# Attention and a two-layer FFN on one core: the first four pairs of heads by 128-partition scores, mask products and transposes, in a new table of steps

## The chip, the core and the metric

One core of one Trainium2 chip. The metric is the device time of one execution, in microseconds (us); lower is better. The engines: PE is TensorE, which multiplies matrices and loads its weights ahead; DVE (VectorE), ACT (ScalarE) and POOL (GpSimd) work element by element; SP issues loads and stores. The on-chip memories are SBUF and, for results of TensorE, eight banks of PSUM.

## The reference

B, H, S, D = 8, 8, 576, 64. Heads 0 to 3 attend to the 32 latest positions, heads 4 to 7 to every fourth of the 128 latest.

```python
scores = scale * np.matmul(q, k.transpose(0, 1, 3, 2))          # scale = 1/8
mask_plain = (rel >= 0) & (rel < window)                        # window 32
mask_dil = (rel >= 0) & (rel < window * dilation) & (rel % dilation == 0)
scores = np.where(masks[None, :, :, :], scores, -1000000000.0)
attn = np.exp(scores - np.max(scores, axis=-1, keepdims=True))
attn = attn / (np.sum(attn, axis=-1, keepdims=True) + 1e-09)
x = np.matmul(attn, v) -> (4608, 512)                           # 4608 tokens, 8 heads x 64
h = x @ w_in                                                    # w_in 512 x 2048
g = np.where(h >= 1, h, np.where(h <= -1, 0.0, (h + 1) ** 2 / 4))
return g @ w_out                                                # w_out 2048 x 512
```

## The kernel before

**Attention.** The 64 heads of the batch are 32 pairs; a pair's 128 rows are one chunk c of the 512 columns of x. The queries of a head stand in 18 blocks of 32, each against 64 keys. For a pair, 36 matmuls (72 instructions) make the scores (S, L179), on 96 partitions by 768 elements; DVE adds the mask (`mask`, L188 to L210); then come the maximum (`max`, L221, DVE), its subtraction (`sub`, L225, POOL), the exponential (`exp`, L229, ACT), the sum (`sum`, L232, DVE), plus epsilon (`eps`, L236, ACT), the reciprocal (`rcp`, L240, DVE) and the product with it (`mul`, L244, POOL). The probabilities are transposed, for pairs 0, 1 and 3 by 12 plain matmuls with a unit matrix (T, L275) that ACT copies out of PSUM (`cp`, L285), for the others by DVE (`tr`, L258), and multiplied with the values (V: 36 matmuls for pairs 0, 1 and 3, L314; 12 of 128 keys for the others, L324).

**The FFN.** x is split into a high and a low part (`hi`, ACT, L295; `lo`, DVE, L299), as is each weight. A tile is 512 tokens; there are 9, each of 16 chunks f of 128 hidden columns. Layer 1 makes h of a chunk by 12 products of 128x128 by 512 (L458: four chunks c by high-high, low-high, high-low); then clamp (DVE, L468), square (`sq`, ACT, L474), larger of the two (`mx`, DVE, L478), high part `gh` (ACT, L485) and low part `gl` (DVE, L490); layer 2 adds 12 products into acc (L504; `o`).

**Weights** come in eight blocks of w_in and eight of w_out, wi0 to wi7 and wo0 to wo7, of two chunks each, as raw 64-bit words (1024 KB a load). ACT takes their top bytes (B, L423) and the scaled rest (P, L416), DVE joins them (J, L429), ACT casts the high part (D, L436) and POOL subtracts for the low part (E, L440).

**Order.** Everything up to the ninth pair and the first tile is written out by hand in the table FIRST: a step's name, its pair or chunk, and its part; each engine and SP runs its own instructions in that order. `const` steps are filler products on TensorE whose results nobody reads. Each raw load or pair's load is an entry of SP's queue: a pair's queries and keys are 592 KB, values 576 KB (L127) or 384 KB (L131), the mask 252 KB. From the tenth pair on a loop over chunks sets the order. BANKS gives the PSUM banks that steps of early pairs write; steps without an entry (S0, S3, V2) take the two banks called `att`. A step that writes a bank waits until the last reader of what stood there is done.

Of the kernel before, what the change touches and what calls it, by code (L numbers as in the profile page):

```python
# [37 lines left out]
lo2.0 h1.0l hi3.0 h0.0h hi3.2 h0.0l hi2.1 lo3.2 h0.1h hi3.1 lo2.1 lo3.0 P.wo0 h0.1l h0.2h lo3.1
h0.2l h0.3h D.wi1 J.wo0 h0.3l S4 qk5 raw.wo1 raw.wi3 raw.wo2 raw.wi4 raw.wo3 raw.wi5 raw.wo4 hi3.3
B.wi2 clamp0 E.wi1 h1.1h h1.1l lo3.3 h1.2h mask4 sq0 h1.2l h1.3h D.wo0 mx0 h1.3l h2.h max4 gh0 P.wi2  # L40
gl0 sub4 h2.l clamp1 h3.h sq1 J.wi2 exp4 mx1 E.wo0 D.wi2 h3.l sum4 gh1 o0.a clamp2 eps4 rcp4 sq2 gl1
mul4 o0.b P.wo1 mx2 h4.h clamp3 E.wi2 gh2 tr4.20 sq3 tr4.11 o1.a B.wo1 gl2 mx3 o0.c J.wo1 h4.l gh3
o1.b gl3 D.wo1 tr4.00 B.wi3 h5.h E.wo1 clamp4 tr4.21 P.wi3 tr4.10 h5.l tr4.01 sq4 J.wi3 o2.a P.wo2
mx4 B.wo2 V4 clamp5 D.wi3 o3.a J.wo2 hi4.0 E.wi3 o2.b hi4.1 lo4.0 hi4.2 gh4 lo4.1 lo4.2 sq5 gl4 S5
qk6 raw.wo5 raw.wi6 raw.wi7 raw.wo6 raw.wo7 D.wo2 mx5 h6.h mask5 B.wo3 E.wo2 max5 h6.l gh5 B.wi4 gl5
o3.b sub5 clamp6 P.wi4 h7.h exp5 J.wi4 P.wo3 h7.l sum5 sq6 o4.b J.wo3 eps5 D.wi4 rcp5 o5.b mx6 mul5
D.wo3 clamp7 o4.a gh6 E.wi4 B.wo4 gl6 o5.a tr5.21 sq7 tr5.01 B.wi5 E.wo3 h8.h mx7 tr5.10 gh7 tr5.00
# [16 lines left out]
def body(ctx, tc, qk, v, v2, mask, w_in, w_out, out):  # L64
# [77 lines left out]
    def constants(count, at):  # L142

        ones, wide = half_t.broadcast_to([128, 128]), half_t.broadcast_to([128, TOK])
        for _ in range(count):
            PE.matmul(out=at, lhsT=ones, rhs=wide, start=True, stop=True)  # L146
# [156 lines left out]
    def values(n, banks=None):  # L303
        hd = heads[n]
        half = NB // 2
        both, ops = banks_of(banks, f"o{n}")
        if n in EARLY:
            for i in range(half):
                for turn in range(2):
                    for part in range(2):  # L310
                        j = part ^ turn
                        r = slice(64 * part, 64 * part + 64)
                        at = 3 * (i // 3 * 2 + j) + i % 3
                        PE.matmul(  # L314
                            out=ops[part][64 * j : 64 * j + 64, QB * i : QB * i + QB],
                            lhsT=hd["v"][r, at],
                            rhs=hd["pt"][r, QB * at : QB * at + QB],
                            start=True,
                            stop=True,
                        )  # L320
        else:
            for t in range(NB // 3):
                for j in range(2):
                    PE.matmul(  # L324
# [381 lines left out]
```

## Time and profile before

| | us |
|---|---|
| median of 3 runs | 889.78 (888.92 to 890.01) |
| the profiled execution | 889.96 |
| its span in the profile | 888.2 |
| TensorE busy, of the span | 876.3 (99%) |
| DVE busy | 545.8 (61%) |
| ACT busy | 306.1 (34%) |
| POOL busy | 133.4 (15%) |
| first product of layer 1 starts | 32.73 |

The span is what the hardware profiler saw from the first instruction to the last; 1.76 us of the execution lie around it. Engines are busy side by side, so their shares do not add up; a busy TensorE may still run at a lower clock, which the profile gives as a granted clock (1.00 is 2.4 GHz, 0.50 is 1.2 GHz).

### The profile page before, as it was taken

The page shows a single profiled execution, that of the slowest core. Times are in us where ns is not written, and L with a number is a line of the kernel's source. Part 1 is how long each engine was busy: PE and PEld are TensorE (multiplying, and loading weights), DVE is VectorE, ACT ScalarE, POOL GpSimd, SP SyncE. Part 2 cuts the span into 40 slices and gives each one's busy share as a digit, 9 for nine tenths or more (in the row PEclk, how much of TensorE's full clock was granted, in tenths as well). Part 3 has the DMA queues.
Part 4 walks back from the last instruction along what each step waited for, and adds up shares of the span by engine and source line. Part 5 has one row for each costly group of instructions (what it writes and reads, how often), then busy time and mean ns, then how long its engine had stood idle before and what let it go on. Part 6 is the DMA issues. An engine that isn't in the chain of part 4 may idle for free.

```text
span 888.2 us, 15897 instructions
## 1 busy us (share of the span) xinstructions
PE 876.3 (99%) x6854; PEld 714.6 (80%) x6854; DVE 545.8 (61%) x865; ACT 306.1 (34%) x496; POOL 133.4 (15%) x84
## 2 busy tenths in 40 slices
PE   7999999999999999999999999999999999999998
PEld 4778878888888888888888888888888888888886
DVE  5799887666766666666666676666666443334333
ACT  3688643322322232232332332223223222222222
POOL 4455441101011111111110101111111000000000
PEclk9899999999999999999999999999999999999999
DMA  9577112101201021101210120102110010001001
GB/s 358 219 283 289 42 64 76 63 28 61 79 20 46 28 99 42 63 29 63 76 63 28 64 75 16 50 28 96 44 64 1 1 47 1 1 1 48 1 1 47
DMA packets 16885, 60.05 MB, mean 68 GB/s; under 512 B 1872, under 2 KB 1872, under 8 KB 14768
## 3 DMA queue, kind: packets, MB, share of 16 engines
q1 hardware_dynamic: 16816, 59.05, 18.4%
q8 instruction: 53, 0.87, 0.4%
q14 instruction: 16, 0.13, 0.0%
HBM read 49.61 MB, written 9.44 MB: 66 GB/s over the span
## 4 chain that ended last, share of the span: by engine, by line
PE 95%; DVE 2%; DMA 1%; POOL 1%; issue 1%; ACT 0%; SPq 0%; POOLq 0%; ACTq 0%
PE acc L504 44%; PE h L458 43%; PE os L337 3%; PE s L179 2%; PE os L179 1%; DMA wi_first<-qk_in 1%; PE o L324 1%; PE consts L146 1%; DVE m_wi L429 0%; DVE m_wo L429 0%; PE t L275 0%; DVE c L221 0%; POOL wi_first L244 0%; DVE gl L490 0%; DVE h L478 0%
## 5 line engine op out<-in xcount | busy, mean ns | idle before, releaser
L504 PE MATMUL acc<-wo,gh 128*128 128x512 f32 x1152 | 381.9, 392 | 0.0
L458 PE MATMUL h<-xh,wi 128*128 128x512 f32 x1152 | 358.2, 390 | 0.9 <-ACT y L474 0.7
L504 PEld LDWEIGHTS acc<-wo,gh 128*128 128x128 f32 x1152 | 216.1, 188 | 47.8 <-DVE gl L490 0.5
L458 PEld LDWEIGHTS h<-xh,wi 128*128 128x128 f32 x1152 | 216.0, 188 | 47.8 <-DVE gl L490 1.1
L504 PE MATMUL acc<-wo,gl 128*128 128x512 f32 x576 | 224.3, 389 | 0.0
L458 PE MATMUL h<-xl,wi 128*128 128x512 f32 x576 | 224.2, 389 | 0.0
L474 ACT ACTIVATE y<-y,small 128x512 f32<-128x512 f32 x144 | 104.2, 724 | 310.5 <-DVE y L468 310.3
L468 DVE TENSOR_SCALAR y<-h 128x512 f32<-128x512 f32 x144 | 99.1, 688 | 114.4 <-PE h L458 111.6
L478 DVE TENSOR_TENSOR h<-h,y 128x512 f32<-128x512 f32 x144 | 100.5, 698 | 98.4 <-ACT y L474 98.4
L490 DVE TENSOR_TENSOR gl<-h,gh 128x512 fp32r<-128x512 f32 x144 | 99.2, 689 | 54.9 <-ACT gh L485 53.3
L458 PEld LDWEIGHTS h<-xl,wi 128*128 128x128 f32 x576 | 108.2, 188 | 22.5
L504 PEld LDWEIGHTS acc<-wo,gl 128*128 128x128 f32 x576 | 108.2, 188 | 21.8
L485 ACT CAST gh<-h 128x512 fp32r<-128x512 f32 x144 | 84.5, 587 | 102.3 <-DVE h L478 99.7
L225 POOL TENSOR_TENSOR c<-c 96x768 f32<-96x768 f32 x29 | 42.7, 1473 | 443.5 <-DVE c L221 443.4
L258 DVE STREAM_TRANSPOSE pts<-c 32x384 f32<-32x384 f32 x168 | 95.3, 568 | 2.9 <-POOL c L244 0.4
L244 POOL TENSOR_TENSOR c<-c 96x768 f32<-96x768 f32 x30 | 44.2, 1473 | 76.2 <-DVE c L240 76.2
L232 DVE TENSOR_REDUCE c<-c 96x12 f32<-96x768 f32 x30 | 28.4, 947 | 38.8 <-ACT c L229 38.8
L229 ACT ACTIVATE c<-c 96x768 f32<-96x768 f32 x30 | 25.4, 845 | 46.8 <-POOL c L225 39.2
L295 ACT CAST xh<-os 128x384 fp32r<-128x384 f32 (+7 forms) x48 | 19.2, 400 | 42.0 <-DVE c L201 21.9
L337 PEld LDWEIGHTS os<-pts,v 128*64 128x64 f32 x576 | 24.5, 137 | 8.5 <-DVE gl L490 6.3
L337 PE MATMUL os<-pts,v 128*64 128x96 f32 x576 | 29.1, 250 | 0.0
L221 DVE TENSOR_REDUCE c<-c 96x12 f32<-96x768 f32 x30 | 28.3, 943 | 0.4
(81 smaller groups left out, 388.4 us busy)
## 6 DMA issues: line engine op xcount, KB each, us to landing
qk<-qk_in SPq DMA_DIRECT2D x29, 592.0 KB, 3.9
v<-v_in SPq DMA_DIRECT2D x28, 384.0 KB, 5.1
raw_wi<-w_in SPq DMA_DIRECT2D x8, 1024.0 KB, 10.6
raw_wo<-w_in SPq DMA_DIRECT2D x8, 1024.0 KB, 12.3
out<-out SPq DMA_DIRECT2D x32, 256.0 KB, 2.1
wi_first<-qk_in SPq DMA_DIRECT2D x2, 592.0 KB, 7.6
out<-outs SPq DMA_DIRECT2D x4, 256.0 KB, 2.0
wo_first<-qk_in SPq DMA_DIRECT2D x1, 592.0 KB, 9.1
```

Of the source, the lines that this page charges most:

```text
L225: engine.tensor_tensor(out=c, in0=c, in1=spread(n, 0), op=ALU.subtract)
L232: nc.vector.tensor_reduce(out=heads[n]["st"][:, 1], in_=heads[n]["c"], op=ALU.add, axis=AX.X)
L244: nc.gpsimd.tensor_tensor(out=c, in0=c, in1=spread(n, 2), op=ALU.mult)
L258: nc.vector.transpose(out=pt[r : r + 32, :, 32 * g : 32 * g + 32], in_=c[32 * g : 32 * g + 32, :, 32 * h : 32 * h + 32],)
L337: PE.matmul(out=at[64 * j : 64 * j + 64, 96 * t : 96 * t + 96], lhsT=hd["v"][:, j, t], rhs=pts[:, j, t], start=True, stop=True,)
L458: PE.matmul(out=hp, lhsT=weight("wi", f, w, slice(128 * c, 128 * c + 128)), rhs=xtile(t)[x][:, c], start=start and (c, w, x) == terms[0], ...
L468: nc.vector.tensor_scalar(out=gs[t, f][0], in0=hps[t, f], scalar1=-1.0, scalar2=1.0, op0=ALU.max, op1=ALU.min)
L474: nc.scalar.activation(out=y, in_=y, func=AF.Square, bias=half_t, scale=0.5)
L478: done.append([nc.vector.tensor_tensor(out=hp, in0=hp, in1=gs[t, f][0], op=ALU.max)])
L485: done[-1].insert(0, nc.scalar.copy(out=g_tile("gh", t, f), in_=hps[t, f]))
L490: nc.vector.tensor_tensor(out=g_tile("gl", t, f), in0=hp, in1=gh.bitcast(F32), op=ALU.subtract)
L504: PE.matmul(out=acc[m], lhsT=g[:, 128 * m : 128 * m + 128], rhs=weight("wo", f, w, slice(0, DM)), start=f == 0 and i == 0, stop=f == NF - ...
```

## The change

For the first four pairs, which all end before the first product of layer 1:

- The scores lie on 128 partitions in three groups of 192 elements, 576 per partition instead of 768 (`early_scores`). Three matmuls of a unit matrix with a mask table (`pm`) write the mask into PSUM first, and the scores are added onto it there. The table with the unit matrix (`tab0`, `tab1`) is loaded ahead of the pairs; the old mask comes later (`late`).
- DVE takes the maximum and subtracts it, straight from PSUM, in two or three operations per pair; `eps` is on DVE, and for pair 3 the product `mul3.v` too.
- T is six matmuls in TensorE's transpose mode, of 128 rows each, copied out by three operations (four of them on ACT, eight on DVE).
- V is 12 matmuls over 128 keys for every early pair; the rows of the transposed table that hold no key are set to zero at the start (seven memsets on DVE). The values are 384 KB for each pair.
- FIRST is another table. From V5 and D.wi5 on its steps stand as before; ahead of that, loads, fillers, attention of pairs 0 to 5, the splitting of x and the first chunks are in another order. o1.a now stands ahead of h4.h.

The core of the diff (of the table one line):

```diff
-EARLY = (0, 1, 3)
+EARLY = 4
...
-S0 const1.5 qk4 mask0 S1 max0 sub0 S2 const1.5 mask1.0 exp0 mask1.1 S3 const1.5 max1 mask2.1
+tab0 qk0 qk1 small49 fill2.5 fill2.5 pm0 pm1 S0 S1 max0 max1.0 max1.2 max0.1 sub0 sub0.1 max1.1 exp0
...
+    def filling(columns, at):
+
+        wide = half_t.broadcast_to([128, 128 * columns])
+        PE.matmul(out=at[:, : 128 * columns], lhsT=wide[:, :128], rhs=wide, start=True, stop=True)
...
+    def place_of(j, b):
+
+        t, r = divmod(b, 3)
+        rr = (1, 0, 2)[r]
+        return (2 * j, rr, t) if t < 4 else (1, rr, 2 * j + t - 4)
+
+    def early_tiles(n):
+
         hd = heads[n]
         if "c" not in hd:
-            hd["c"] = pool.tile([96, 832], F32, tag="c", name=f"c{n}", bufs=2)
+            hd["c"] = pool.tile([128, 832], F32, tag="c", name=f"c{n}", bufs=2)
         cc = hd["c"]
+        hd["wide"] = cc[:, :672].rearrange("p (k x) -> p k x", k=3)
+        hd["c"] = hd["wide"][:, :, QB:].rearrange("p k (r x) -> p k r x", x=KW)
+        hd["st"] = cc[:, 672:699].rearrange("p (s k r) -> p s k r", s=3, k=3)
+        nc.vector.memset(hd["wide"][:, :, :QB], 0.0)
+        if n:
+            nc.vector.memset(hd["pts"], 0.0)
+            hd["pts"] = hd["pts"].rearrange("p (u x) -> p u x", x=96)
+        else:
+            hd["pts"] = pts.rearrange("p j t x -> p (j t) x")
+
+    def early_scores(n):
+        hd = heads[n]
+        sps = hd["s"][1]
+        for j, b in [(j, 3 * t + r) for t in range(6) for r in range(3) for j in range(2)]:
+            k, rr, g = place_of(j, b)
+            r = slice(64 * j, 64 * j + 64)
+            PE.matmul(
+                out=sps[k][QB * g : QB * g + QB, KW * rr : KW * rr + KW],
+                lhsT=hd["q"][r, QB * b : QB * b + QB],
+                rhs=hd["k"][r, QB * b : QB * b + KW],
+                start=False,
+                stop=True,
+                skip_group_check=True,
+            )
...
+    def masks_first(n, banks=None):
+
+        hd = heads[n]
+        both, (one, two) = banks_of(banks, f"s{n}")
+        hd["s"] = both, (one, bank(4 + n % 2, f"sc{n}"), two)
+        ident, m = tables[0][:, :128], tables[n // 2][:, 0 if n // 2 else 128 :]
+        rest = m[:, :KW].unsqueeze(1).broadcast_to([128, 3, KW]) if n < 2 else m[:, 3 * KW :]
+        for sp, rhs in zip(hd["s"][1], (m, rest, m)):
+            o = sp[:, : 3 * KW]
+            PE.matmul(
+                out=o.rearrange("p (a x) -> p a x", x=KW) if len(rhs.shape) > 2 else o,
+                lhsT=ident, rhs=rhs if len(rhs.shape) > 2 else rhs[:, : 3 * KW],
+                start=True, stop=False, skip_group_check=True,
+            )
+
+    def halves(n, k):
+        both, sps = heads[n]["s"]
+        if k is None:
+            return slice(0, 3, 2), both[:, :, : 3 * KW].rearrange("p k (r x) -> p k r x", x=KW)
+        r, src = slice(k, k + 1), sps[k][:, : 3 * KW].unsqueeze(1)
+        return r, src.rearrange("p k (r x) -> p k r x", x=KW)
...
+    def largest(n, k=None):
+        r, src = halves(n, k) if n < EARLY else (slice(0, 2), heads[n]["c"])
+        nc.vector.tensor_reduce(out=heads[n]["st"][:, 0, r], in_=src, op=ALU.max, axis=AX.X)
+
+    def minus_largest(n, k=None):
         c = heads[n]["c"]
-        engine.tensor_tensor(out=c, in0=c, in1=spread(n, 0), op=ALU.subtract)
+        if n < EARLY:
+            r, src = halves(n, k)
+            nc.vector.tensor_tensor(out=c[:, r], in0=src, in1=spread(n, 0)[:, r], op=ALU.subtract)
+            return
+        nc.gpsimd.tensor_tensor(out=c, in0=c, in1=spread(n, 0), op=ALU.subtract)
...
     def epsilon(n):
         st = heads[n]["st"]
+        if n < EARLY:
+            nc.vector.tensor_scalar(out=st[:, 1], in0=st[:, 1], scalar1=EPS, scalar2=None, op0=ALU.add)
+            return
...
-    def divided(n):
+    def divided(n, engine=nc.gpsimd):
         c = heads[n]["c"]
-        nc.gpsimd.tensor_tensor(out=c, in0=c, in1=spread(n, 2), op=ALU.mult)
+        engine.tensor_tensor(out=c, in0=c, in1=spread(n, 2), op=ALU.mult)
...
     def transpose_pe(n, banks):
...
+
+        hd, ident = heads[n], tables[0][:, :128]
+        tps = hd["t"] = banks_of(banks, f"t{n}")[1]
+        for k in range(3):
+            for side, x in enumerate((hd["wide"][:, k, 96:], hd["wide"][:, k, :96])):
+                PE.transpose(tps[side][: x.shape[1], 128 * k : 128 * k + 128], x, ident)
+
+    def copied(n, r, engine=None):
+        rows = (slice(0, 64), slice(0, 96), slice(64, 128))[r]
+        src = heads[n]["t"][r % 2][rows, :384].rearrange("p (u x) -> p u x", x=QB)
+        dst = heads[n]["pts"][rows, :, QB * r : QB * r + QB]
+        if engine:
+            nc.vector.tensor_copy(out=dst, in_=src)
+        else:
+            nc.scalar.copy(out=dst, in_=src)
...
-        half = NB // 2
         both, ops = banks_of(banks, f"o{n}")
...
+        for t in range(NB // 3):
+            for j in range(2):
+                if n < EARLY:
+                    x = hd["pts"][:, t + (0, 8 if t < 4 else 2)[j]]
+                else:
+                    x = pts[:, j, t]
+                PE.matmul(
+                    out=ops[t // 3][64 * j : 64 * j + 64, 96 * (t % 3) : 96 * (t % 3) + 96],
+                    lhsT=hd["v"][:, j, t],
+                    rhs=x,
+                    start=True,
+                    stop=True,
+                )
         hd["o"] = list(pieces(n, both, ops))
...
-    BANKS = {"S1": (0, 1), "S2": (2, 3), "T0": (0, 1), "T1": (2, 3), "T3": (0, 1), "V0": (4, 5), "V1": (2, 3), "V3": (2, 3)}
+    BANKS = {"S1": (0, 1), "S2": (2, 3), "T0": (0, 1), "T1": (2, 3), "T2": (0, 1), "T3": (0, 1), "V0": (4, 5), "V1": (2, 3), "V3": (2, 3)}
+    QUEUES = {None: nc.sync, "a": nc.scalar}
...
+        "tab": lambda i: nc.sync.dma_start(
+            out=tables[int(i)], in_=mask4[:, 320 * int(i) : 320 + 384 * int(i)]
+        ),
+        "late": lambda _: nc.sync.dma_start(out=small[:96, : 9 * KW], in_=mask),
...
+    for n in range(EARLY):
+        heads[n] = {}
+    for n in range(1, EARLY):
+        heads[n].update(first_batch(n))
+    for n in range(EARLY):
+        early_tiles(n)
```

**SP, the loads.** From the start of the program, before and now. wi_first, wo_first, xl_first and xh_first are places of later weights and of x in which early pairs lie; 128x1184 is a pair's queries and keys, 128x2048 a weight block, v or 128x768 and 128x1152 values.

```order
L120 DMA qk_68<-qk_in 128x1184
L603 DMA small<-mask_in 96x672
L120 DMA wi_first<-qk_in 128x1184
L120 DMA wi_first_74<-qk_in 128x1184
L120 DMA wo_first_77<-qk_in 128x1184
L127 DMA v_80<-v_in 128x1152
L403 DMA raw_wi_82<-w_in 128x2048
L127 DMA wo_first<-v_in 128x1152
L131 DMA xh_first_75<-v_in 128x768
L127 DMA xl_first_78<-v_in 128x1152
```

```order
L639 DMA wi_first_68<-mask_in 128x320
L117 DMA qk_86<-qk_in 128x1184
L117 DMA wi_first_68<-qk_in 128x1184
L124 DMA xl_first_73<-v_in 128x768
L124 DMA wo_first_69<-v_in 128x768
L639 DMA wi_first_68<-mask_in 128x384
L117 DMA wi_first_70<-qk_in 128x1184
L124 DMA v_250<-v_in 128x768
L117 DMA xh_first_72<-qk_in 128x1184
L449 DMA raw_wi_370<-w_in 128x2048
L449 DMA raw_wi_456<-w_in 128x2048
L124 DMA wo_first_71<-v_in 128x768
```

Behind the pairs' loads stood one pair's values and the first weights; now the mask tables and three pairs' values stand ahead of the fourth pair, and both blocks of w_in before v2.

**DVE, the end of the early attention.** From the reciprocal of pair 1 to the splitting of x before, and from pair 3's maximum on now. wi_first_74 was pair 2 and wo_first_77 pair 3; now wi_first_70 is pair 2 and xh_first_72 pair 3. COPY rows are copies of transposes out of PSUM.

```order
L240 RECIPROCAL c_187<-c_187 96x12
L210 TENSOR_TENSOR wo_first_77<-s_271,small 96x768
L221 TENSOR_REDUCE wo_first_77<-wo_first_77 96x12
L232 TENSOR_REDUCE wi_first_74<-wi_first_74 96x12
L240 RECIPROCAL wi_first_74<-wi_first_74 96x12
L429 SCALAR_TENSOR_TENSOR m_wi_338<-m_wi_338,raw_wi_82 128x1024
L232 TENSOR_REDUCE wo_first_77<-wo_first_77 96x12
L240 RECIPROCAL wo_first_77<-wo_first_77 96x12
L258 STREAM_TRANSPOSE pts<-wi_first_74 32x12x32 x6
```

```order
L279 TENSOR_TENSOR xh_first_72<-s_288,xh_first_72 128x2x192
L279 TENSOR_TENSOR xh_first_72<-sc_289,xh_first_72 128x192
L288 TENSOR_REDUCE wi_first_70<-wi_first_70 128x9
L293 TENSOR_SCALAR wi_first_70<-wi_first_70 128x9
L341 COPY wo_first_69<-t_2_358 64x12x32
L299 RECIPROCAL wi_first_70<-wi_first_70 128x9
L288 TENSOR_REDUCE xh_first_72<-xh_first_72 128x9
L341 COPY wo_first_69<-t_2_358 64x12x32
L293 TENSOR_SCALAR xh_first_72<-xh_first_72 128x9
L299 RECIPROCAL xh_first_72<-xh_first_72 128x9
L341 COPY wo_first_69<-t_3_359 96x12x32
L303 TENSOR_TENSOR xh_first_72<-xh_first_72 128x3x192
```

The mask's addition went; subtraction, epsilon, the copies and pair 3's product came to DVE, and J.wi0 (L429, now L475) stands behind them all.

**DVE, the first chunks.** From the join of wo0 before, and from the clamp of chunk 0 now. L468/L514 is clamp, L299/L357 lo, L429/L475 J, L478/L524 mx, L203/L251 mask4, L221/L273 max4, L490/L536 gl, L288 sum4.

```order
L429 SCALAR_TENSOR_TENSOR m_wo_573<-m_wo_573,raw_wo_89 128x1024
L468 TENSOR_SCALAR y_0_642<-h_0_561 128x512
L299 TENSOR_TENSOR xl_483<-o_3_513,xh_482 128x16x2
L203 TENSOR_TENSOR c_586<-s_587,small 96x768
L478 TENSOR_TENSOR h_0_561<-h_0_561,y_0_642 128x512
L221 TENSOR_REDUCE c_586<-c_586 96x12
L490 TENSOR_TENSOR gl_0_674<-h_0_561,gh_0_670 128x512
L468 TENSOR_SCALAR y_1_681<-h_1_555 128x512
L429 SCALAR_TENSOR_TENSOR m_wi_672<-m_wi_672,raw_wi_405 128x1024
L478 TENSOR_TENSOR h_1_555<-h_1_555,y_1_681 128x512
```

```order
L514 TENSOR_SCALAR y_0_522<-h_0_486 128x512
L357 TENSOR_TENSOR xl_428<-o_3_473,xh_427 128x16x2
L357 TENSOR_TENSOR xl_428<-o_459,xh_427 128x64
L475 SCALAR_TENSOR_TENSOR m_wo_530<-m_wo_530,raw_wo_506 128x1024
L524 TENSOR_TENSOR h_0_486<-h_0_486,y_0_522 128x512
L251 TENSOR_TENSOR c_545<-s_546,small 96x768
L273 TENSOR_REDUCE c_545<-c_545 96x12
L536 TENSOR_TENSOR gl_0_606<-h_0_486,gh_0_601 128x512
L514 TENSOR_SCALAR y_1_608<-h_1_489 128x512
L475 SCALAR_TENSOR_TENSOR m_wi_603<-m_wi_603,raw_wi_527 128x1024
L524 TENSOR_TENSOR h_1_489<-h_1_489,y_1_608 128x512
L288 TENSOR_REDUCE c_545<-c_545 96x12
```

J.wo0 moved from ahead of the clamp of chunk 0 to behind it and behind two lo steps; J.wi2 stands ahead of mx1 as before.

## Rows read from the trace of the kernel before

**Rows 1.** The page's chain that ended last, share of the span by line.

```profile
PE acc L504 44%; PE h L458 43%; PE os L337 3%; PE s L179 2%; PE os L179 1%; DMA wi_first<-qk_in 1%; PE o L324 1%; PE consts L146 1%; DVE m_wi L429 0%; DVE m_wo L429 0%; PE t L275 0%; DVE c L221 0%; POOL wi_first L244 0%; DVE gl L490 0%; DVE h L478 0%
```

**Rows 2.** The stretches view: start:end, length, then each engine's busy time, granted clock, DMA.

```profile
32.73:47.75 15.02, 14.36 (x138) 11.38 (x130) 13.27 (x19) 11.34 (x20) 6.96 (x4) 1.00 0.63 247
...
60.00:600.00 540.00, 539.76 (x4354) 441.57 (x4352) 363.81 (x585) 191.09 (x312) 94.00 (x57) 1.00 0.18 62
```

**Rows 3.** The chain in order of time (start, length, what), from 33 us on.

```profile
40.97 3.90 DVE m_wi L429
...
54.47 2.72 PE h L458 x12
...
58.55 1.14 PE o L324 x24
```

**Rows 4.** The same chain up to the first h product.

```profile
18.34 1.17 PE t L275 x24
...
24.63 1.34 PE t L275 x17
...
26.23 0.91 PE t L275 x7
27.14 2.02 PE consts L146 x2
...
29.20 2.19 PE o L324 x24
...
32.80 3.62 PE h L458 x15
```

**Rows 5.** The stretches view around the start of the h stream.

```profile
26.00:31.00 5.00, 4.71 (x31) 2.92 (x32) 3.54 (x8) 1.78 (x4) 0.90 (x1) 0.50 0.58 226
31.00:32.00 1.00, 1.00 (x37) 0.78 (x34) 0.00 (x0) 0.57 (x2) 0.00 (x0) 0.56 0.00 0
32.00:33.00 1.00, 1.00 (x57) 0.96 (x50) 0.69 (x1) 1.00 (x3) 0.00 (x0) 1.00 0.00 0
```

**Rows 6.** The timeline of TensorE (start, length, line, out<-in, count, idle before): scores.

```profile
8.82 0.97 PE L179 MATMUL s<-wi_first 64*32 64x64 f32 x72 [1.13 <-DMA wi_first<-qk_in]
10.26 0.97 PE L179 MATMUL s<-wi_first 64*32 64x64 f32 x72 [0.47 <-DMA wi_first<-qk_in]
```

**Rows 7.** The timeline of DVE.

```profile
6.67 0.95 DVE L203 TENSOR_TENSOR c<-s,small 96x768 f32<-96x768 f32 x1 [5.81 <-PE s L179]
...
11.73 0.54 DVE L201 TENSOR_TENSOR wi_first<-s,small 96x384 f32<-96x384 f32 x1
...
16.93 0.22 DVE L240 RECIPROCAL c<-c 96x12 f32<-96x12 f32 x1 [1.49 <-ACT c L236]
...
21.59 0.94 DVE L232 TENSOR_REDUCE wo_first<-wo_first 96x12 f32<-96x768 f32 x1
...
28.99 1.22 DVE L429 SCALAR_TENSOR_TENSOR m_wi<-m_wi,raw_wi 128x1024 uint32<-128x1024 uint32 x1
...
36.47 0.69 DVE L468 TENSOR_SCALAR y<-h 128x512 f32<-128x512 f32 x1 [0.36 <-PE h L458]
```

**Rows 8.** The groups of DVE by line and form, 60 to 600 us.

```profile
L299 DVE TENSOR_TENSOR xl<-os,xh 128x192 fp32r<-128x192 f32 x8 | 2.8, 356 | 1.5 <-ACT xh L295 1.5
```

**Rows 9.** The timeline of POOL.

```profile
20.67 2.32 POOL L244 TENSOR_TENSOR wi_first<-wi_first 96x768 f32<-96x768 f32 x1 [0.17 <-DVE wi_first L240]
...
39.95 1.47 POOL L225 TENSOR_TENSOR c<-c 96x768 f32<-96x768 f32 x1 [1.58 <-DVE c L221]
41.38 2.41 POOL L440 TENSOR_TENSOR wo<-m_wo,wo 128x1024 fp32r<-128x1024 f32 x1
```

**Rows 10.** The timeline of ACT.

```profile
32.98 0.87 ACT L295 CAST xh<-o 128x256 fp32r<-128x256 f32 x4
33.68 1.17 ACT L416 ACTIVATE m_wo<-raw_wo 128x1024 f32<-128x1024 f32 x1
34.72 1.07 ACT L436 CAST wi<-m_wi 128x1024 fp32r<-128x1024 f32 x1
```

More of the change, by code (lines that the diff above doesn't have):

```diff
@@ L38 @@
[L38 to L47, printed above, removed]
@@ new lines @@
+sub2.0 sum1 sub2.1 eps1 sub2.2 rcp1 exp2 mul1 qk3 S3 max3 max3.1 sub3 sub3.1 T0 cp0.0 cp0.2 T1 exp3
+cp0.1 sum2 eps2 raw.wi0 B.wi0 fill3.att cp1.0.v rcp2 mul2 sum3 cp1.2.v eps3 rcp3 cp1.1.v mul3.v V0
+T2 V1 P.wi0 J.wi0 hi0.1 hi0.0 hi0.2 cp2.2 hi1.2 hi1.0 D.wi0 E.wi0 cp2.0.v cp2.1.v T3 lo0.2 lo1.0
+hi1.1 cp3.0.v cp3.2.v cp3.1.v lo1.2 lo1.1 lo0.1 lo0.0 raw.wi1 v2 V2 V3 h0.0h h1.0h B.wi1 hi3.2 hi3.0
+P.wi1 hi2.0 hi3.1 hi3.3 hi2.1 lo3.0 lo3.2 J.wi1 lo3.1 lo2.0 raw.wo0 h0.0l h1.1l h0.1l h0.2l h0.1h
@@ new lines @@
+h0.3h h1.3h h1.0l h0.2h h0.3l clamp0 B.wo0 lo3.3 lo2.1 raw.wi2 B.wi2 P.wo0 J.wo0 D.wi1 sq0 E.wi1
+h1.2l D.wo0 v4 qk4 S4 h1.1h h1.2h h1.3l h2.h late mx0 mask4 max4 gh0 P.wi2 sub4 gl0 clamp1 J.wi2
+E.wo0 h2.l h3.h o0.a h3.l o0.b raw.wo1 raw.wo3 B.wo3 sq1 exp4 mx1 sum4 clamp2 gh1 D.wi2 eps4 rcp4
+gl1 mul4 E.wi2 o1.a h4.h sq2 P.wo1 mx2 gh2 clamp3 sq3 B.wo1 gl2 o0.c o1.b h4.l mx3 gh3 J.wo1 D.wo1
+E.wo1 gl3 h5.h h5.l o2.a tr4.10 tr4.21 tr4.20 clamp4 tr4.11 tr4.00 tr4.01 raw.wi6 V4 o2.b o3.a
+raw.wo4 raw.wi3 raw.wo2 qk5 B.wi3 P.wi3 sq4 J.wi3 P.wo2 B.wo2 J.wo2 mx4 D.wi3 E.wi3 hi4.2 hi4.0
@@ new lines @@
+hi4.1 lo4.1 clamp5 lo4.0 lo4.2 S5 raw.wi4 raw.wo7 raw.wi7 raw.wo6 raw.wi5 raw.wo5 qk6 gh4 gl4 h6.h
+h6.l sq5 D.wo2 mx5 mask5 max5 E.wo2 sub5 B.wi4 gh5 P.wi4 P.wo3 clamp6 gl5 o3.b o4.a o4.b h7.h h7.l
+J.wi4 J.wo3 B.wi5 exp5 D.wi4 sq6 E.wi4 sum5 mx6 B.wo4 gh6 gl6 clamp7 h8.h o5.b h8.l o5.a D.wo3 eps5
+rcp5 mul5 E.wo3 P.wi5 sq7 mx7 tr5.20 tr5.01 tr5.10 tr5.11 o6.b J.wi5 P.wo4 gh7 B.wo5 o6.a clamp8
+tr5.00 tr5.21 gl7 D.wi5 V5 v6 J.wo4 sq8 h9.h E.wi5 hi5.2 mx8 hi5.0 hi5.1 lo5.0 gh8 lo5.1 D.wo4 h9.l
@@ L63, in body @@
 @with_exitstack
-def body(ctx, tc, qk, v, v2, mask, w_in, w_out, out):
+def body(ctx, tc, qk, v, mask, mask4, w_in, w_out, out):
     nc = tc.nc
@@ L136, in load_v @@
             for i in range(2):
-                nc.sync.dma_start(out=both[:, i].rearrange("p j t d -> p (j t d)"), in_=v2[n + i - len(EARLY)])
+                nc.sync.dma_start(out=both[:, i].rearrange("p j t d -> p (j t d)"), in_=v[n + i])
                 heads.setdefault(n + i, {})["v"] = both[:, i]
     last, done = {}, []
[L142 to L146, printed above, removed]
+    def filling(columns, at):
+        wide = half_t.broadcast_to([128, 128 * columns])
+        PE.matmul(out=at[:, : 128 * columns], lhsT=wide[:, :128], rhs=wide, start=True, stop=True)
     def small_constants(count, ats):
@@ L304, in values @@
         hd = heads[n]
-        half = NB // 2
         both, ops = banks_of(banks, f"o{n}")
[L307 to L324, printed above, removed]
-                        out=ops[t // 3][64 * j : 64 * j + 64, 96 * (t % 3) : 96 * (t % 3) + 96],
-                        lhsT=hd["v"][:, j, t],
-                        rhs=pts[:, j, t],
-                        start=True,
-                        stop=True,
-                    )
+        for t in range(NB // 3):
+            for j in range(2):
+                if n < EARLY:
+                    x = hd["pts"][:, t + (0, 8 if t < 4 else 2)[j]]
+                else:
+                    x = pts[:, j, t]
[6 more added lines that the diff above has]
+                )
         hd["o"] = list(pieces(n, both, ops))
```

144 lines of the change are left out of this document (59 added, 85 removed).

## The prediction

> **What bounds the kernel now.** I read the page's chain first: TensorE's products of the two layers, acc and h, make 87% of it [rows 1]. The stretches say where TensorE still idles. From the first h product at 32.73 us to 47.75 it is busy 14.36 of 15.02 us, and between 60 and 600 us all but 0.24 [rows 2]. So the time is the start of the h stream, plus a fixed amount of TensorE work, plus what the stream stalls. Only steps up to V5 are moved, so a gain can come only from the first 33 us, and be given back only in the stream's first stretch. There, 57 products stand before 47.75. Twelve take 2.72 us further on [rows 3], that is 0.227 each; 57 x 0.227 + S4 0.9 = 13.8, so before loses 1.2 us there.
>
> The chain of the first 33 us ends with the transposes of the fourth pair (24.63 to 27.14), filler products (2.02 us), V2 (2.19), V3, and h [rows 4]. V4, the same 24 instructions as V2, takes 1.14 us [rows 3]: V2 ran at half clock. The granted clock is 0.50 from 26 to 31 us (the 1.2 GHz level) and 1.00 again from 32, less than a microsecond ahead of h [rows 5].
>
> **The fourth pair arrives later.** Scores of pairs 1 and 2 started as their loads came, 1.44 us apart for 592 KB: 411 KB/us [rows 6]. At 10.26 us 2028 KB had come. In the new order of loads 3872 KB end with pair 3's: 10.26 + 1844 / 411 = 14.75. It is 3 us later than before, yet before made little of it: T0, next behind S3, began at 18.34 [rows 4]. S3 takes about a microsecond, as S1 did [rows 6]: 15.75. The mask's three products per pair wait for no pair's load and lie under it; bare, three of 192 columns would be 1.1 us at the price of the half-clock fillers (2.02 for two of 512 [rows 4]). The seven memsets on DVE have the idle 5.81 us ahead of 6.67 [rows 7]; they cost 3 x 1.55 + 4 x 0.2 = 5.4 at the price of 128x512 elements (0.69, so 1.55 for 1152) and stay covered, barely.
>
> **DVE then sets the pace**, fourteen operations up to pair 3's product. By the nearest rows: five of 384 elements from PSUM at 0.54 (2.70), two of 192 at 0.36 [rows 8] (0.72), three of 576 at three quarters of 0.94 (2.12), four small ones at 0.22 (0.88) [rows 7]: 6.4. Rows start 0.09 before the previous ends: less 1.2. For hand-overs I add 0.6: 5.8, ending at 21.6. J.wi0 (1.22 [rows 7]) and two copies of pair 2 (0.54 each) follow, since T3 writes the banks they read: 23.7. Of the transposes T3 alone is on the path: T2 starts when mul2 ends on POOL, near 20 by the same count, and J.wi0 covers it. **Its six transposes are the unknown price.** T0 before, 12 plain products of 96 columns, took 1.17 us at full clock [rows 4]; six of 128 are two thirds of its columns, 0.8. From below I let them go at a quarter of that, 0.2, as nothing excludes a faster mode; from above they take what T3 itself took before at the falling clock, 1.34 + 0.91 = 2.3 [rows 4]. I take 0.9, near the row at full clock: 24.6. Three copies of 0.54 less overlap: 26.0. V2 runs beneath them, V3 after: 27.2 at full clock (1.14 each [rows 3]), 29.0 at half clock (2.19 each [rows 4]). The clock fell before where TensorE waited for one pair's end, and it still waits there, so I take a value near the low one: **28.4, against 32.73: 4.3 us gained.** The filler of 2.02 on the old path is part of that: the new one stands earlier, ahead of V0.
>
> The Trainium skill, "TensorE: Matmul & The Clock Gate", Terms, calls transpose mode four times faster for FP32; its Part 4 measured about 275 ns for one 128x128 transpose, in bf16, in a kernel. By the first, the sum would be about 0.7 better; by the second, an estimate of 1.65 us for six, 0.75 worse. No row of before holds such an instruction.
>
> **What is given back.** Two waits.
> First S4. It now stands behind 18 products of h0 and h1 and one more, 4.3 us. It needs the bank of pair 2's values, which lo2.1 frees; lo2.1 stands on DVE behind clamp0, and clamp0 behind h0's end: 28.4 + 18 x 0.227 = 32.5. Clamp0 0.69 [rows 7], two small lo steps: 33.5. TensorE is there at 32.7: 0.9 lost.
> Second o1.a, now ahead of h4.h. DVE runs J.wo0 (to 34.6), mx0, mask4, max4, gl0, clamp1 (at 0.6 to 0.86 apart by [rows 7], 0.95 and 0.94 for the mask and the maximum) to 38.1, then J.wi2. POOL has sub4 from 37, and E.wo0 queued behind. In before the same J took 3.90 us on the chain [rows 3]: it reached DVE during sub4 (39.95 to 41.42) and came through only when the next POOL operation had ended too (43.8) [rows 9]. I price it so: 42.0. Then mx1, gh1 on ACT: 43.3; gl1 behind sum4, clamp2 and rcp4, which waits for eps4 behind D.wi2 on ACT: 45.3. TensorE reaches o1.a at 33.6 + S4 0.9 + 29 h products 6.6 + 9 acc products 2.0 = 43.1; it waits 0.2 for gh1 and 1.8 for gl1. Some twelve hand-overs at 0.05 are not in this chain: 0.6 more, 2.6 in all.
> 0.9 + 2.6 less the 1.2 that before lost: 2.3 given back. DVE's added eps, the POOL product that went to DVE and the 12 rather than 36 matmuls of V are inside the terms above. Later raw loads (wi6 and wo3 early, wi4, wi5 late) land many us before use by the 411 KB/us; I price them at nothing, and if the queue runs late, h6 waits.
>
> **Sum:** -4.3 + 2.3 = -2.0, with rounding of the terms -1.9. The profiled execution took 889.96, 0.18 above the median of the runs: **888.1**. Against the median that is -1.7, just inside 0.2% (1.78 us), which is about what a measurement can tell from no change. The case's own range is -2.9 to -0.9.
>
> **Rivals.**
> *J.wo0 loses the port (slower).* DVE reaches J.wo0 at 33.5. POOL's E.wi1 starts when D.wi1 ends on ACT: casts of V2 and V3 about 1.4 (four took 0.87), then B.wo0, B.wi2, P.wo0 and D.wi1 at 1.07 to 1.17 [rows 10], 0.09 less each: from 28.4 to 34.0. J wins by half a microsecond, and E.wi1 waits for it, as mul2 did at 20.67 (2.32 instead of 1.47 [rows 9]). If TensorE runs the first h products at half clock for over a microsecond (clock rises late, as it rose only 0.8 us ahead of h before), h0's end slips, ACT does not, and E.wi1 (2.41) goes first: J.wo0 and all that follows on DVE comes 2.5 to 3 later, with the slip itself: net +0.8 to +3.0. For it: the thin margin and the low clock. Against: ACT's chain is long and may slip too.
> *Dear transposes.* T3 at 2.3, or as much again for a clock that stays low through it, 3.7: 1.4 to 2.8 later for everything: net -0.5 to +0.9, no change.
> *The clock holds* (the gaps between S3, T and V are shorter than before): h at 27.2, net -3.0.
> *J.wi2 waits for sub4 alone.* Then it ends at 39.7, o1 waits for nothing: net -4.3. The 3.90 of [rows 3] speaks against it. The Trainium skill, "SBUF — State Buffer", § SBUF: two separate sides, has whoever starts first hold the shared pair of ports for its whole instruction; by that rule a waiting J would have its turn after sub4. In [rows 3, 9] J let two POOL operations pass.
> *The start was never the bound:* if wi1 and wo0, which land no sooner than before, set h2's start, all is given back, net 0. By the loads, wi1 has come at 20 and wo0 at 23.5, so I leave it with the dear transposes.
>
> **Chances.** Forecast 0.36 (about half of it beyond -1.78), port lost 0.28 (0.17 of it beyond +1.78), dear transposes or the start no bound 0.13, clock holds 0.13, sub4 alone 0.10. Faster: 0.19 + 0.13 + 0.10 = 0.42; same: 0.17 + 0.11 + 0.13, rounded to 0.40; slower 0.18. The range leaves out sub4 alone and the worst of the port case: -3.5 to +2.3, 886.5 to 892.3.
>
> **What would show it.** First h product at 27.2 to 29.0 at a clock below or just back at 1.00; T3's rows 0.2 to 2.3 in all; DVE without idle from S3's end to pair 3's product; TensorE idle before S4 about 0.9, before o1.a about 2.6; J.wi2 near 3.9 us behind two POOL operations. Wrong if J.wo0 is the long one, if h starts after 30, or if TensorE idles elsewhere up to V5.

## The result and the profile after

| | before | changed |
|---|---|---|
| median, us | 889.78 (888.92 to 890.01) | 897.47 (897.09 to 897.74) |
| span of the profiled execution, us | 888.2 | 895.9 |
| first product of layer 1 starts | 32.73 | 28.08 |

The ratio of the changed kernel to before is 1.0088, 95% interval 1.007 to 1.0105: 0.9% slower, where -0.2% was forecast and the range ended at +0.3%.

The chain of the changed kernel up to the first h product answers to [rows 4] (start, length, what):

```profile
16.59 0.68 DVE xh_first L273 x2
...
21.59 0.74 DVE xh_first L303
22.33 0.51 DVE m_wi L475
...
23.39 1.02 DVE wo_first L341 x2
...
24.45 0.65 PE t L334 x4
...
26.90 1.24 PE o L370 x24
28.13 4.58 PE h L504 x18
```

DVE runs from pair 3's maximum (16.59) to its product (21.59), J.wi0 and two copies, then T3, V3 and h: the chain that the prediction wrote down, and h starts within 0.3 us of it. The nine traces that keep this order up to h, this one and eight of the experiments, start it between 27.09 (e3) and 28.19 (e10), so differences of up to 1.1 us in that start can be chance. The stretches around it answer to [rows 5]; the granted clock (1.00 behind POOL's busy time) did not fall:

```profile
25.00:26.00 1.00, 1.00 (x22) 0.87 (x22) 0.85 (x2) 0.87 (x1) 1.00 (x1) 1.00 1.00 392
26.00:31.00 5.00, 4.45 (x46) 3.34 (x41) 4.24 (x11) 3.34 (x8) 1.00 (x1) 1.00 1.03 353
31.00:32.00 1.00, 1.00 (x5) 0.82 (x5) 0.34 (x1) 1.00 (x2) 0.00 (x0) 1.00 1.01 426
```

TensorE's two waits in the stream are there as well, in its timeline (the last bracket is the idle time before a row):

```profile
33.76 0.96 PE L205 MATMUL s<-qk 64*32 64x64 f32 x72 [0.83 <-issue]
...
45.52 0.50 PE L550 MATMUL acc<-wo,gl 128*128 128x512 f32 x1 [1.36 <-DVE gl L536]
```

So 4.6 us were gained and 2.2 waited for, and yet the span is 7.7 longer. The chain far behind the moved steps shows where they went. There both kernels run the same instructions in the same order, twelve products to a row; before, then now:

```profile
761.84 2.72 PE acc L504 x12
764.56 2.72 PE h L458 x12
```

```profile
762.27 2.73 PE acc L550 x12
765.00 2.79 PE h L504 x12
...
773.32 2.74 PE acc L550 x12
776.06 2.73 PE h L504 x12
...
786.98 2.73 PE h L504 x12
789.71 2.80 PE acc L550 x12
```

Before, such a row takes 2.72 us in either layer. Now layer 1 takes 2.79 until 776, then 2.73; layer 2 takes 2.73, and 2.80 where layer 1's fast rows end. TensorE idles nowhere in these rows: in a slow one each product is issued 2.6% later after the one before it (2.79 against 2.72). The last 36 products, before and now:

```profile
876.08 8.17 PE acc L504 x36
```

```profile
883.70 8.38 PE acc L550 x36
```

From the first h product to the end of these rows before takes 876.08 + 8.17 - 32.73 = 851.5 us, the changed kernel 883.70 + 8.38 - 28.08 = 864.0: 12.5 more, on the same products.

### The profile page after: what moved, and what is told of

Its sections match the earlier page's. It is cut to its first block, busy times and chain, and to the rows that moved or that the text cites. A ratio compares the mean times of both kernels' runs of the same rounds, so it can differ in the third digit from the quotient of the medians.

```text
span 895.9 us, 15568 instructions
## 1 busy us (share of the span) xinstructions
PE 885.3 (99%) x6680; PEld 716.7 (80%) x6680; DVE 546.4 (61%) x888; ACT 305.0 (34%) x490; POOL 126.7 (14%) x80
## 4 chain that ended last, share of the span: by engine, by line
PE 95%; DVE 4%; issue 0%; ACT 0%; POOL 0%; POOLq 0%
PE acc L550 44%; PE h L504 43%; PE os L383 3%; PE os L205 2%; PE s L205 1%; PE o L370 1%; DVE m_wo L475 1%; DVE m_wi L475 0%; DVE gl L536 0%; DVE c L273 0%; PE s L184 0%; PE fill L138 0%; PE s L223 0%; PE small L145 0%; DVE wo_first L341 0%
## 5 line engine op out<-in xcount | busy, mean ns | idle before, releaser
L504 PE MATMUL h<-xh,wi 128*128 128x512 f32 x1152 | 362.4, 394 | 0.2
L504 PE MATMUL h<-xl,wi 128*128 128x512 f32 x576 | 227.0, 394 | 0.0
L514 DVE TENSOR_SCALAR y<-h 128x512 f32<-128x512 f32 x144 | 99.2, 689 | 125.3 <-PE h L504 124.2
L524 DVE TENSOR_TENSOR h<-h,y 128x512 f32<-128x512 f32 x144 | 100.5, 698 | 99.4 <-ACT y L520 99.4
L536 DVE TENSOR_TENSOR gl<-h,gh 128x512 fp32r<-128x512 f32 x144 | 99.3, 690 | 55.1 <-ACT gh L531 53.5
L281 POOL TENSOR_TENSOR c<-c 96x768 f32<-96x768 f32 x28 | 41.2, 1472 | 439.2 <-DVE c L273 438.8
L303 POOL TENSOR_TENSOR c<-c 96x768 f32<-96x768 f32 (+1 forms) x30 | 43.5, 1450 | 87.9 <-DVE c L299 87.9
L288 DVE TENSOR_REDUCE c<-c 96x12 f32<-96x768 f32 (+1 forms) x30 | 28.0, 933 | 38.8 <-ACT c L285 38.8
L285 ACT ACTIVATE c<-c 96x768 f32<-96x768 f32 (+1 forms) x30 | 25.0, 834 | 49.0 <-POOL c L281 38.7
L205 PE MATMUL s<-qk 64*32 64x64 f32 x1188 | 27.0, 220 | 0.8 <-issue 0.8
```

The lines of the kernel that those rows point to most:

```text
L205: PE.matmul(out=sps[j][QB * g : QB * g + QB, KW * t : KW * t + KW], lhsT=hd["q"][r, QB * b : QB * b + QB], rhs=hd["k"][r, QB * b : QB * b ...
L281: nc.gpsimd.tensor_tensor(out=c, in0=c, in1=spread(n, 0), op=ALU.subtract)
L303: engine.tensor_tensor(out=c, in0=c, in1=spread(n, 2), op=ALU.mult)
L504: PE.matmul(out=hp, lhsT=weight("wi", f, w, slice(128 * c, 128 * c + 128)), rhs=xtile(t)[x][:, c], start=start and (c, w, x) == terms[0], ...
L514: nc.vector.tensor_scalar(out=gs[t, f][0], in0=hps[t, f], scalar1=-1.0, scalar2=1.0, op0=ALU.max, op1=ALU.min)
L524: done.append([nc.vector.tensor_tensor(out=hp, in0=hp, in1=gs[t, f][0], op=ALU.max)])
```

## The experiments

**Which products are slow.** Weight blocks 6 and 7 belong to chunks 12 to 15 of a tile, four rows of 16, and that is how many fast rows layer 1 has and slow ones layer 2. The programs' SBUF addresses separate them. Setting up the early pairs, the changed code claims the places of w_in and w_out 6, 7 and of x ahead of the tile `qk`, whose 4736 bytes are 18.5 times 256; before, `qk` was claimed ahead of them all. Offsets of the tiles modulo 256 bytes, worked out from the sizes of the tiles in the order in which the programs claim them (what counts here is their differences), with the rows:

| | x | w_in 0-5 | w_in 6-7 | g (gh, gl) | w_out 0-5 | w_out 6-7 |
|---|---|---|---|---|---|---|
| before | 128 | 128 | 128 | 128 | 128 | 128 |
| changed | 128 | 0 | 128 | 0 | 0 | 128 |
| 12 products, changed, us | | 2.79 with x | 2.73 with x | | 2.73 with g | 2.80 with g |

By the table neither offset is slow by itself: 0 with 0 and 128 with 128 are fast, 0 with 128 is slow either way round. Theory A: products are slow where the weights that are loaded and the operand that is streamed lie at different offsets. Rival B: the PSUM banks, which the change allocates in another order; rival C: the clock or the chip. e1 and e3 add unused bytes behind a tile and change no instruction:

```diff
-            hd["qk"] = pool.tile([128, S + KPAD], F32, tag="qk", name=f"qk{n}")
+            hd["qk"] = pool.tile([128, S + KPAD + 96], F32, tag="qk", name=f"qk{n}")[:, : S + KPAD]
```

> The changed kernel with 96 unused floats behind each pair's tile of queries and keys, so that w_in and w_out, g and the scratch tiles lie 384 bytes further in SBUF, at 128 modulo 512 like x; no instruction and no order changes. Theory A (place of operands: a product is slow when the weights loaded and the operand streamed differ modulo 256 bytes): 12 products of layer 1 take 2.72 us instead of 2.79, the span falls by about 9.7 us, to some 887.7 us, 2 below before. Rival B (the other order of PSUM banks): no change, 897.5. Rival C (the clock or the chip's power at this pace): no change, 897.5.

Measured: 886.58 us (886.26 to 886.84), ratio to before 0.9977 (0.9966 to 0.9988). The chain has 2.72 everywhere again:

```profile
764.25 2.72 PE acc L550 x12
766.97 2.72 PE h L504 x12
...
777.85 2.72 PE h L504 x12
```

The last 36 products of e1, then of e3:

```profile
873.05 8.17 PE acc L550 x36
```

```profile
872.01 8.17 PE acc L550 x36
```

From e1's first h product (27.29) to the end of the last 36 is 873.05 + 8.17 - 27.29 = 853.9 us; in e3, whose first stands at 27.09, it is 853.1. Of the 12.5 us that the stream was longer than before, 10.1 by e1 and 10.9 by e3 were the place of the tiles, and 2.4 or 1.6 are the order of work.

e2 does the reverse to the kernel before:

```diff
-            both = pool.tile([128, 1536], F32, tag="v", name=f"v{n}")
+            both = pool.tile([128, 1536 + 32], F32, tag="v", name=f"v{n}")[:, :1536]
```

(and the same for the early pairs' values).

> The kernel before with 32 unused floats behind each tile of values: w_in blocks 0 to 5, w_out blocks 0 to 5 and g move to 0 modulo 256 bytes, while x and blocks 6 and 7 stay at 128; PSUM banks and order stay. Theory A: the same two classes as in the changed kernel, about 10 us slower, 899 to 900. Rivals B and C: 889.8.

Measured: 899.54 (897.88 to 901.14), ratio 1.0127 (1.0109 to 1.0146). The rows are those of the changed kernel:

```profile
765.10 2.79 PE h L458 x12
767.89 2.73 PE acc L504 x12
...
776.16 2.73 PE h L458 x12
...
789.81 2.80 PE acc L504 x12
```

B and C fall: PSUM is as before here, and the tiles' places alone make the kernel before as slow as the changed one (899.54 and 897.47). How far apart may they be? e3 adds 32 floats, e4 16, e10 40 in the line of e1's diff.

> The changed kernel with 32 unused floats there: weights 0 to 5 and g at 384 modulo 512, x at 128, so equal modulo 256 and 256 apart modulo 512. Theory A as stated (modulo 256): fast, 887.7. If what matters is modulo 512: still slow, 897. Rivals B and C: 897.5.

> The changed kernel with 16 unused floats there: weights 0 to 5 and g at 64 modulo 256, x at 128, so 64 bytes apart. Theory A has no number for it: 897 if any difference modulo 256 costs, 887.7 if only 128 does; between if the cost goes with the distance. Rivals B and C: 897.5.

> The changed kernel with 40 unused floats behind each pair's queries and keys: weights 0 to 5 and g at 160 modulo 256, x and blocks 6 and 7 at 128, so 32 bytes apart. If any distance within 256 bytes costs: 892 to 898, as 64 (894.4) and 128 (897.5) bytes did. If only steps of 64 bytes matter: 886.3.

| weights 0-5 and g from x, modulo 512 bytes | median, us | ratio to before (95%) |
|---|---|---|
| 0 (e1) | 886.58 | 0.9977 (0.9966 to 0.9988) |
| 256 (e3) | 886.34 | 0.9971 (0.996 to 0.9983) |
| 128 (changed kernel) | 897.47 | 1.0088 (1.007 to 1.0105) |
| 192, 64 from the next 256 (e4) | 894.37 | 1.0063 (1.005 to 1.0077) |
| 288, 32 from 256 (e10) | 899.96 | 1.013 (1.0116 to 1.0145) |

Equal modulo 256 is enough; 32 bytes cost the most, more than the 892 to 898 expected, so the cost does not go with the distance. Rows of e4, then of e10:

```profile
764.85 2.77 PE acc L550 x12
767.62 2.76 PE h L504 x12
...
778.65 2.76 PE h L504 x12
```

```profile
764.50 2.75 PE acc L550 x12
767.25 2.80 PE h L504 x12
```

In both, layer 2 is slower than 2.72 too, though w_out 0 to 5 and g keep equal offsets. In e4 so is layer 1 in chunks 12 to 15 (the row at 778.65), where w_in 6, 7 and x lie at 128 both. So what is shown is that the tiles' places make the loss, that places equal modulo 256 bytes avoid it, and that at 128 bytes apart it falls on the products whose two operands differ; at 64 and 32 bytes apart theory A does not say which rows lose, and that stays open. So does the mechanism inside TensorE: the durations of the weight loads did not change (188 ns in both kernels' pages).

**Are the two waits worth what they last?** e5 to e9 start from e3's kernel (886.34) and change only the table.

```diff
 e5  -... clamp0 B.wo0 lo3.3 lo2.1
     +... lo3.3 lo2.1 clamp0 B.wo0
 e6  -... clamp1 J.wi2 E.wo0 ... sq1 exp4 mx1 sum4 clamp2 gh1 D.wi2 eps4 rcp4 gl1 mul4
     +... clamp1 E.wo0 ... sq1 mx1 J.wi2 exp4 gh1 gl1 sum4 clamp2 D.wi2 eps4 rcp4 mul4
 e8  -... J.wi0 hi0.1 hi0.0 hi0.2 cp2.2 hi1.2 hi1.0 D.wi0 E.wi0 cp2.0.v cp2.1.v T3
     +... hi0.1 hi0.0 hi0.2 cp2.2 hi1.2 hi1.0 cp2.0.v cp2.1.v J.wi0 D.wi0 E.wi0 T3
 e9  -... mx1 J.wi2 exp4 gh1 gl1 sum4 clamp2 D.wi2 ... sq2 P.wo1 mx2 gh2
     +... mx1 clamp2 J.wi2 exp4 gh1 sq2 gl1 mx2 sum4 D.wi2 gh2 ... P.wo1
```

e7 is e5 and e6 together, e8 and e9 add theirs to e7.

> Against the changed kernel with the 128-byte pad (886.3): lo3.3 and lo2.1 stand ahead of clamp0 on DVE. Theory (S4 waits for pair 2's bank behind clamp0): the 0.8 us before S4 go, S4 starts at the end of h1.2l. But o1.a waits for the chain clamp0, J.wo0, ..., J.wi2, gl1, which gains only the two small operations (0.3), so its wait grows: about 0.3 us in all, 886.0. Rival (S4's wait is worth what it lasts): 885.5.

> Against the same 886.3: mx1 stands ahead of J.wi2 on DVE, gl1 straight behind it, gh1 ahead of sum4. Theory (o1.a waits for gl1 behind a J.wi2 that waits for two POOL operations): J.wi2 ends no later than now (42.4 in the changed kernel, as E.wo0 ends at 41.3 in any case), and the 1.4 us before o1.a's gl1 go: 885.0. Rival (J.wi2, later on DVE, makes h4 or h4.l late): 886 or more.

> Both edits, against the same 886.3. Theory: with o1.a no longer late, S4's wait counts in full: -0.8 and -1.4, at most 0.4 of it lost to h4.l waiting for E.wi2: 884.3. Rival (they share one cause): 885.0, as with mx1 alone.

> Both edits, and J.wi0 moved behind the two copies of pair 2 that T3 waits for. Theory (T3 waits 1.05 us for those copies, which stand behind J.wi0 of 1.2): the first h product comes 0.7 us earlier, and as nothing ahead of o1 is late, 0.7 of it reaches the end: 883.6. Rival (E.wi0 ends 1.1 later and h0's low products wait for it, or chunk 2's weights now come late): 884.3 or more.

> Against the run with both edits (885.9): clamp2 stands ahead of J.wi2 on DVE, in the time in which J.wi2 waits for POOL, and sq2, mx2, gh2 follow as soon as they can. Theory (in the run with both edits the wait at o1 went to gl2, which acc waits 1.2 us for, as DVE is the bound from clamp0 to gl2; one operation out of the time behind J.wi2 shortens that chain): gl2 ends 1 us or more earlier, 884.9. Rival (DVE's sum of work up to V4 sets the end of that stretch, not the order): the wait goes on to gl3 or S5, 885.9.

| | median, us | ratio to before (95%) |
|---|---|---|
| e5, lo first | 886.68 (886.11 to 888.17) | 0.9976 (0.9965 to 0.9986) |
| e6, mx1 first | 886.25 (885.65 to 887.71) | 0.9972 (0.9963 to 0.9982) |
| e7, both | 885.89 (885.26 to 886.36) | 0.9965 (0.9955 to 0.9976) |
| e8, and J.wi0 | 886.49 (886.13 to 886.72) | 0.997 (0.9961 to 0.998) |
| e9, and clamp2 | 886.98 (886.28 to 887.8) | 0.9985 (0.9976 to 0.9994) |

None of the intervals parts from e3's. e6 removed the wait for gl1 and was to give 1.3 us; it gave 0.1. In e5 the 0.8 before S4 went and 0.7 before o1.a, for gh1, came, as its theory had it; its profiled execution (887.99) also shows a mean granted clock of 0.57 from 46 to 50 us, behind these 0.7 and the 1.4 for gl1, and the three slowest of its ten (887.9 to 888.2) are those with a mean clock of 0.998. In e8 T3's wait fell from 1.1 to 0.6 and V3's, behind J.wi0 and pair 3's copies, rose from 0.6 to 1.4. The waits of TensorE in e6, e7 and e9 (engine and line, what it waited for, total us, times, longest) say where they went:

```profile
PE s L205 <- issue: 1.2, 2, 0.8
...
PE acc L550 <- DVE gl L536: 0.8, 1, 0.8
```

```profile
PE acc L550 <- DVE gl L536: 1.2, 1, 1.2
...
PE s L205 <- issue: 0.3, 1, 0.3
```

```profile
PE h L504 <- DVE gl L536: 0.6, 2, 0.5
...
PE h L504 <- POOL wi L486: 0.4, 1, 0.4
PE s L205 <- issue: 0.3, 1, 0.3
```

In e6 acc waits for gl2 instead, and S4 and S5 wait too; in e7 gl2 alone takes 1.2; in e9, where gl2 is in time, layer 1 waits for a later gl and for POOL's weight block, and S5 waits again. The waits change their name, and their sum falls by less than was expected: from 2.2 us in e3 to 2.0, 1.5 and 1.3. e7's chain shows why (start, length, what):

```profile
40.33 0.78 DVE m_wi L475
41.11 1.25 issue
42.36 0.68 DVE gl L536
...
46.84 0.70 DVE gl L536
```

J.wi2 waits through POOL's E.wo0 and runs until 42.36, gl1, and then one DVE or ACT operation after the other to gl2 at 46.84. Here the engines beside TensorE set the pace, which fits the rival of e9: there J.wi2 comes through in 1.30 us, and J.wo1 behind it takes 2.49 instead of 1.22. That no order could do better is not shown, and e9's 886.98, on another chip, is 1.1 above its rival's number, which stays unexplained. My price of those waits had assumed that TensorE was the bound behind them.

**Are the fillers needed?**

```diff
-tab0 qk0 qk1 small49 fill2.5 fill2.5 pm0 pm1 S0 S1 ...
+tab0 qk0 qk1 pm0 pm1 S0 S1 ...
-cp0.1 sum2 eps2 raw.wi0 B.wi0 fill3.att cp1.0.v ...
+cp0.1 sum2 eps2 raw.wi0 B.wi0 cp1.0.v ...
```

> The changed kernel with the 128-byte pad (886.3), without its filler products (small49, both fill2.5, fill3.att). Theory (the clock stayed at 1.00 up to the h stream because TensorE is kept busy, by the fillers among others): the granted clock falls to 0.50 somewhere in the first 33 us, T, V or the first h products run at the low clock, and the time is 1 to 3 us longer, 887.3 to 889.3, with a wider spread. Rival (the mask products and the transposes keep it busy enough alone, the fillers do nothing): clock 1.00 throughout, 886.3 or up to 0.3 less.

Measured: 888.29 (887.43 to 888.83), ratio 0.9993 (0.9981 to 1.0005): 2 us slower than e3, as the theory said. Each of its times lies above each of e3's, but the two ran on different chips, and the intervals overlap from 0.9981 to 0.9983. The theory's reason is shown only in part. Its column of granted clock reads 1.00 to the h stream. TensorE's timeline of e11, then of the changed kernel:

```profile
4.58 1.49 PE L223 MATMUL s<-wi_first 128*128 128x192 f32 x4
...
7.28 1.21 PE L184 MATMUL s<-qk 64*32 64x64 f32 x40
...
14.64 0.52 PE L184 MATMUL sc<-wi_first 64*32 64x64 f32 x11 [0.90 <-issue]
...
27.74 1.24 PE L370 MATMUL o<-xl_first 128*64 128x96 f32 x24 [0.55 <-DVE xl_first L341]
```

```profile
6.54 1.20 PE L223 MATMUL s<-wi_first 128*128 128x192 f32 x4
...
14.11 0.59 PE L223 MATMUL s<-wi_first 128*128 128x192 f32 x2
...
15.28 0.82 PE L184 MATMUL s<-xh_first 64*32 64x64 f32 x41
```

Four mask instructions take 1.49 us at 4.58 in e11 and 1.20 at 6.54 in the changed kernel, two take 0.59 at 14.11; forty scores take 1.21 at 7.28, and 41 take 0.82 at 15.28. The column is filled in before the trace's first clock record (5.2 us in e3, 7.3 in the changed kernel, 9.1 in e11), so the first microseconds ran at the lower level, by the rows' durations, although it shows 1.00; without fillers that lasted into S0, and pair 1's first maximum came at 10.00, against 9.24 in e3 but 10.29 in the changed kernel. Then a gap of 0.90 stands in S2 that the profile puts down to issue. e3 has none there, but e7, which has the fillers, has one in S3, so it is not shown to come of their absence, and its cause is open:

```profile
15.60 0.67 PE L184 MATMUL s<-xh_first 64*32 64x64 f32 x32 [0.87 <-issue]
```

V3 started at 27.74 against 25.91 in e3 and 26.9 in the changed kernel and e7. The traces so leave 0.8 to 1.8 us to the missing fillers and that gap together; how much is the clock's stays open.

## Why the prediction was wrong

**The step that failed** is the frame: "the time is the start of the h stream, plus a fixed amount of TensorE work, plus what the stream stalls". The TensorE work was not fixed. The same 3456 products took 10.1 to 10.9 us more, because the change, by claiming tiles in another order, moved blocks 0 to 5 and g by 128 bytes modulo 256 against x. No row of before could show it, as there all offsets were equal; the order of the instructions does not show it either. Only the tiles' addresses do, and the prediction left them out. None of the rivals held this case, and so the range ended 5 us short.

**The terms of the sum** held, some by luck:
- Start of h: 28.4 forecast, 28.08 measured, 27.09 to 28.19 over the traces with this order. DVE's fourteen operations: 5.8 forecast, 5.7 measured (16.59 to 22.33). S3 started at 15.28 rather than 14.75, because pm3 stood on the path: I had priced the mask products at nothing, and here they cost half a microsecond. V2 and V3 ran at full clock, 1.24 where I had taken a value near 2.19, which gave that back.
- T3: 0.9 forecast; T0's six instructions took 0.87, and four of T3's stand at 0.65 in the chain. The dear transposes fall. The Trainium skill, "TensorE: Matmul & The Clock Gate", Terms, calls transpose mode four times faster for FP32; this trace does not agree, as the six were no cheaper than the 0.8 forecast for plain products.
- S4's wait: 0.9 forecast, 0.83. o1.a's: 2.6 forecast, 1.36 for gl1; J.wi2 went as priced. Its rows, on DVE and then POOL's:

```profile
33.57 1.22 DVE L475 SCALAR_TENSOR_TENSOR m_wo<-m_wo,raw_wo 128x1024 uint32<-128x1024 uint32 x1
...
38.40 3.98 DVE L475 SCALAR_TENSOR_TENSOR m_wi<-m_wi,raw_wi 128x1024 uint32<-128x1024 uint32 x1
```

```profile
34.18 2.88 POOL L486 TENSOR_TENSOR wi<-m_wi,wi 128x1024 fp32r<-128x1024 f32 x1 [7.18 <-ACT wi L482]
37.46 1.47 POOL L281 TENSOR_TENSOR c<-c 96x768 f32<-96x768 f32 x1 [0.40 <-DVE c L273]
38.89 2.40 POOL L486 TENSOR_TENSOR wo<-m_wo,wo 128x1024 fp32r<-128x1024 f32 x1
```

J.wi2 reached DVE at 38.40, in sub4 (to 38.93), and came through only after E.wo0 (to 41.29): 3.98 in all, 3.90 of it on the chain, as the 3.90 of before [rows 3, 9]. J.wo0, at 33.57, won against E.wi1 at 34.18, which took 2.88; the rival in which it loses fell by 0.6 us. The Trainium skill, "SBUF — State Buffer", § SBUF: two separate sides, has whoever starts first hold the shared pair of ports for its whole instruction. E.wi1's 2.88, against 2.40 for E.wo0, agrees with it; that J.wi2 waited for a second POOL operation does not follow from it, and the rival in which it waits for sub4 alone fell.
- Net of order, without the offsets: e1 starts h at 27.29 and gives back 2.4, e3 1.6, forecast 2.3; e1's 886.58 lies within the range, 2.6 below before on the same chip where 1.7 was forecast.

The clock held in the changed kernel, which I had given 0.13, and that is most of what the new front is worth. e2's profiled execution shows it: it has the order of before, its granted clock stayed at 1.00 from 8 to 32 us, and its h starts at 29.89, 2.8 us ahead of the 32.73; the new order itself takes it from there to 27.09 to 28.19, 1.7 to 2.8 more. The times agree: among 15 runs of before beside e1, those with a mean granted clock of 0.998 took 886.5 to 887.0 us and those at 0.990 took 889.8 to 890.0. Against those at 0.998 e3's 886.34 is 0.2 to 0.6 better.

**The best version** is e7 by its median: 885.89, ratio 0.9965 (0.9955 to 0.9976), 128 unused bytes and two places in the table away from the change. It beats both kernels; against e3, with the bytes alone, the intervals overlap.

## What to carry to other kernels

When a change touches what is allocated, or in which order, compare the tiles' addresses as well as the instructions: here 128 bytes per partition cost 1.2% through products that the diff does not mention. Where a TensorE that is always busy is slower than before at the same clock, read the time of twelve equal products in both kernels before looking for waits. And a wait on a full engine is worth what it lasts only if the engine waited for has slack behind it.

## What was not expected of the hardware

- A 128x128 by 512 product in a dense stream took 2.72 / 12 = 0.227 us in the kernels in which all weights and streamed operands lie at equal offsets modulo 256 bytes in SBUF (before, e1, e3), and 2.79 / 12 = 0.233 where the two lay 128 bytes apart; with blocks 0 to 5 and g 32 bytes from x modulo 256 the whole kernel took 899.96, with 64 bytes 894.37, and 256 apart 886.34.
- The column of granted clock says 1.00 for the first microseconds, in which the same mask instructions took twice as long as later: in the changed kernel's chain 0.64 us for two at 5.47 and 0.33 for two at 7.74.
- A DVE join that reached its engine while POOL ran one operation (sub4) with another queued behind it (E.wo0) came through only after both, before and now: 3.98 us for a join that takes 1.22 alone.
